# A state-space convolution and a gated unit in one kernel: the idle products of the head cut into halves of 256 columns

## The chip, the cores and the metric

The kernel runs on one core of a Trainium2 chip. A core has five engines that run side by side, each from an instruction stream of its own: TensorE (PE in the profile; its weight loads are listed apart, as PEld), VectorE (DVE), ScalarE (ACT), GpSimd (POOL) and SyncE (SP, which here only issues transfers). Sixteen DMA engines move data between the device's memory and the on-chip memories, and they also bring in the engines' code. TensorE writes its results to PSUM, a memory of eight banks, here two pairs and four single banks.

The metric is the device time of one execution in microseconds (us), the median over several runs. A profiled execution is a run of its own: it has a time, and a span from its first to its last instruction, and all rows of the profile count from the start of that span.

## The reference

Only what fixes the amount of work is shown.

```python
def reference(A_u, A_A_re, A_A_im, A_B_re, A_B_im, A_C_re, A_C_im,
              A_log_dt, A_Dskip, B_x, B_w_gate, B_w_up, B_w_down):
    # x is 1 x 2048 x 512 (bf16), F = 1792, 128 modes per channel
    x = A_u
    xn = _layernorm(x, axis=-1)
    return x + _A_ref(xn, ...) + _B_ref(xn, ...)

def _A_ref(u, ...):
    dt = jnp.exp(log_dt)[:, None]
    logdA = dt * (A_re + 1j * A_im)
    P = jnp.exp(logdA[:, :, None] * l)                # l = 0 .. 2047
    K = jnp.einsum("dn,dnl,dn->dl", Cc, P, dB).real   # one long filter per channel
    ...                                               # causal convolution of u with K by FFT
    return y + u * Dskip

def _B_ref(x, w_gate, w_up, w_down):
    g = jnp.einsum("bsd,df->bsf", x, w_gate)
    u = jnp.einsum("bsd,df->bsf", x, w_up)
    return jnp.einsum("bsf,fd->bsd", _sigmoid(g) * u, w_down)
```

So a normalized input goes through two branches, a long convolution and a gated unit with three matrix products, and both are added to the input.

## The kernel before

**The gated unit.** Its 2048 tokens are worked in four groups of 512. For each group and each of 14 blocks of 128 features there are four products with `wg_sb` (line 1036) and four with `wu_sb` (line 1060), each 128x128 against 512 columns. ScalarE takes the sigmoid and moves the other half out of PSUM (lines 1048 and 1072), VectorE multiplies the two (line 1076). Then, for each 128 tokens, 14 products with `wd_sb` (line 1105) sum into one bank.

**The convolution.** The filter is built from powers of a table on VectorE and ScalarE, and by four bursts of 128 small products on TensorE (line 820, `f_k`, 82 columns each, 64 to a call). The convolution itself is a transform of 2048 = 64 x 32, made by products (lines 694, 882, 904, 926, 985) with two passes through the device's memory in between (`z_scr` and `v_scr`), and pointwise products on VectorE.

**The head.** Four transfers bring the first tokens. VectorE and ScalarE compute the layernorm of the first 512 tokens, TensorE transposes them in two calls of eight (line 564, `ft`), and ScalarE and VectorE copy the transposes to `xnT` (lines 571 and 573). The weights come in by the queue of SyncE, `wg_sb` in three pieces and `wu_sb` in two, with more tokens in between.

**The idle products.** `keep_warm` (lines 516 to 522) adds an operation to TensorE's list that multiplies a zeroed tile, `glu_sb[:, 0, :]`, with itself into a PSUM bank that nobody reads. They compute nothing of the result; they only keep TensorE at work. There are eight such operations: one of 14 products, three of 3, and four of 1. In the order of TensorE stand the 14, a single one and a 3, then the first eight transposes, then a 3 and a single one, then the other eight transposes, then the last 3. Two single ones stand far behind, at 27.8 us and 194.0 us of the profile.

**The order of the work.** Every operation is added to a plan, and a list written out by hand, `ORDER`, gives the order in which the operations are issued; each engine takes its own in that order. PSUM banks and buffers are handed out in the same order. The cost given to `pl.add` is not used where `ORDER` is given. The number and the place of the operations don't depend on how many instructions one of them issues.

**The streams.** Each product is two instructions in TensorE's stream, a weight load and a product. The 1876 products of this kernel make 3752 instructions, and the code is brought in block by block while the kernel runs (queue 8 of the profile, kind "instruction").

Of the kernel before, what the change touches and what calls it, by code (L numbers as in the profile page):

```python
# [317 lines left out]
def kernel(  # L318
# [12 lines left out]
    V, S, T, P, Y = nc.vector, nc.scalar, nc.tensor, nc.gpsimd, nc.sync  # L331
# [12 lines left out]
    def bank(slot, r=0):  # L344
        if slot.pool == "s":
            return pairs[slot.idx][:, 512 * r:512 * r + 512]
        return banks[slot.idx][:]
# [18 lines left out]
    glu_sb = const.tile([128, 8, D], BF, name="glu_sb")  # L366
# [149 lines left out]
    def keep_warm(n, prio):  # L516
        wsl = _Slot("gu")

        def fn():
            for _ in range(n):  # L520
                T.matmul(bank(wsl), glu_sb[:, 0, 0:128], glu_sb[:, 0, :], start=True, stop=True)
        return pl.add("PE", 6.2 if n > 3 else 0.2155 * n, fn, (), prio, acq=[wsl], rel=[wsl])

    keep_warm(14, -10)
# [222 lines left out]
    for c in range(4):  # L747
        PC = PCH[c]
        cs = slice(CW * c, CW * c + CW)
# [9 lines left out]
        n = 1  # L759
# [435 lines left out]
```

## Time and profile before

| what | us |
|---|---|
| three runs | 217.63, 217.75, 219.24 |
| median | 217.75 |
| the profiled execution, its own time | 219.51 |
| its span, first to last instruction | 217.6 |
| TensorE busy | 209.0 |
| VectorE busy | 193.8 |
| ScalarE busy | 179.5 |

The busy times of the table can be read against the span: an engine with 96% has hardly any idle time, though ends of products are modelled, and two products that overlap in the pipeline count once. Between the span and the execution's own time lie 1.9 us before the first and behind the last instruction. The profiled execution was 1.8 us longer than the median of the three runs, so its rows are used for differences and not for the level.

### The profile page before, as it was taken

Reading aid. Unit: us, or ns where it says so; the run is one execution under the profiler, and the core shown is the slowest. Engines: PE = TensorE matmul, PEld = TensorE weight load, DVE = VectorE, ACT = ScalarE, POOL = GpSimd, SP = SyncE. Lnnn points to the kernel's source line nnn. Section 1 sums busy time; section 2 is a strip of 40 time slices with the busy share of each in tenths; the row PEclk is TensorE's granted clock in tenths of the full one; section 3 lists DMA queues with packets and bytes.
Section 4 is the critical chain, followed back from the end, with each engine's and each line's share of the span. In section 5 each row is a group of like instructions: output and inputs, shape, how many; then the busy total and the mean of one; then the engine's idle time right before and its main releaser. Section 6 shows DMA issues by size and latency. Waiting matters only on the chain.

```text
span 217.6 us, 4946 instructions
## 1 busy us (share of the span) xinstructions
PE 209.0 (96%) x1876; PEld 104.0 (48%) x1876; DVE 193.8 (89%) x438; ACT 179.5 (83%) x286; POOL 18.8 (9%) x40
## 2 busy tenths in 40 slices
PE   7979999999999999989999999999999999999894
PEld 2435444444444454435455565445546556544463
DVE  3989999999999999999999999999999999970433
ACT  3799999999999999869989999976897999960111
POOL 1410202002100020012000002010800000000000
PEclk9999999999999999999999999999999999999999
DMA  6999936001463689865697679929959969984974
GB/s 186 316 369 390 299 116 146 0 3 48 145 156 97 233 249 156 264 143 105 166 271 202 183 224 209 239 79 216 216 116 252 282 188 263 267 245 139 269 256 166
DMA packets 51530, 42.80 MB, mean 197 GB/s; under 512 B 16434, under 2 KB 43571, under 8 KB 51507
## 3 DMA queue, kind: packets, MB, share of 16 engines
q1 hardware_dynamic: 50338, 40.60, 63.8%
q0 software_dynamic: 864, 1.57, 5.5%
q10 hardware_dynamic: 304, 0.33, 0.6%
q8 instruction: 14, 0.23, 0.4%
q14 instruction: 10, 0.07, 0.1%
HBM read 25.97 MB, written 12.85 MB: 178 GB/s over the span
## 4 chain that ended last, share of the span: by engine, by line
PE 64%; DMA 17%; ACT 8%; SPq 7%; issue 2%; DVE 0%; ACTq 0%
PE bank L1060 18%; PE bank L1036 16%; PE bank L1105 10%; PE pair L904 7%; SPq L421 7%; DMA wu_sb<-in_B_w_up_dram 5%; PE pair L926 4%; ACT big L287 4%; DMA z_scr<-big 3%; DMA big<-big 3%; DMA big<-z_scr 2%; DMA v_scr<-big 2%; PE pair L882 2%; PE pair L820 2%; ACT us_sb L1072 2%
## 5 line engine op out<-in xcount | busy, mean ns | idle before, releaser
L287 ACT ACTIVATE big<-pair 128x1024 bf16<-128x1024 f32 x64 | 66.2, 1060 | 4.9 <-PE pair L926 1.5
L1060 PE MATMUL bank<-xnT,wu_sb 128*128 128x512 bf16 x224 | 54.5, 380 | 0.5 <-DMA wu_sb<-in_B_w_up_dram 0.4
L1036 PE MATMUL bank<-xnT,wg_sb 128*128 128x512 bf16 (+1 forms) x220 | 50.7, 368 | 1.9 <-DMA wg_sb<-in_B_w_gate_dram 1.8
L1105 PE MATMUL bank<-wd_sb,hT_sb 128*128 128x512 bf16 (+1 forms) x238 | 50.4, 367 | 0.0
L1036 PEld LDWEIGHTS <-wg_sb 128*128 128x128 bf16 x236 | 22.2, 98 | 26.9 <-issue 2.5
L1105 PEld LDWEIGHTS <-hT_sb 128*128 128x128 bf16 x238 | 22.6, 98 | 25.2 <-issue 1.9
L1060 PEld LDWEIGHTS <-wu_sb 128*128 128x128 bf16 x224 | 20.6, 98 | 25.2 <-issue 3.0
L1048 ACT ACTIVATE hT_sb<-bank 128x512 bf16<-128x512 f32 x52 | 30.9, 636 | 1.2 <-PE bank L1036 1.1
L735 DVE TENSOR_TENSOR big<-big 128x1024 bf16<-128x1024 bf16 (+4 forms) x40 | 26.8, 670 | 0.3 <-ACT big L287 0.2
L736 DVE TENSOR_TENSOR big<-big 128x1024 bf16<-128x1024 bf16 (+4 forms) x40 | 26.7, 667 | 0.0
L1072 ACT ACTIVATE us_sb<-bank 128x512 bf16<-128x512 f32 x40 | 25.9, 648 | 0.3
L909 DVE TENSOR_TENSOR big<-big 128x2048 bf16<-128x2048 bf16 x16 | 19.5, 1218 | 0.6 <-PE pair L926 0.3
L904 PE MATMUL pair<-big 128*128 128x256 bf16 x160 | 19.8, 273 | 0.0
L789 ACT ACTIVATE sq_sb<-big 128x256 bf16<-128x256 bf16 (+2 forms) x20 | 13.8, 691 | 5.1 <-DVE big L741 4.9
L904 PEld LDWEIGHTS <-big 128*128 128x128 bf16 x160 | 15.4, 98 | 4.9 <-issue 1.0
L1076 DVE TENSOR_TENSOR hT_sb<-hT_sb,us_sb 128x512 bf16<-128x512 bf16 x40 | 16.5, 418 | 0.4 <-ACT us_sb L1072 0.3
L740 DVE TENSOR_TENSOR big<-big 128x512 bf16<-128x512 bf16 (+4 forms) x40 | 16.5, 414 | 0.1
L741 DVE TENSOR_TENSOR big<-big 128x512 bf16<-128x512 bf16 (+4 forms) x40 | 16.5, 413 | 0.0
L1007 ACT ACTIVATE big<-pair 128x1024 bf16<-128x1024 f32 x3 | 3.1, 1023 | 15.2 <-PE pair L985 12.4
L895 DVE COPY big<-big 32x1024 bf16<-32x1024 bf16 x32 | 13.4, 419 | 0.6
L1011 DVE TENSOR_TENSOR big<-pair,glu_sb 128x1024 bf16<-128x1024 f32 x2 | 2.5, 1226 | 11.7 <-PE pair L985 8.1
L541 DVE BATCH_NORM_STATS2 stats<-big 128x6 f32<-128x512 bf16 x15 | 9.8, 682 | 3.4 <-DMA big<-in_A_u_dram 3.4
(104 smaller groups left out, 244.3 us busy)
## 6 DMA issues: line engine op xcount, KB each, us to landing
big<-c_E SPq DMA_DIRECT2D x16, 320.0 KB, 3.9
z_scr<-big SPq DMA_DIRECT2D x16, 256.0 KB, 2.9
big<-z_scr SPq DMA_DIRECT2D x16, 256.0 KB, 4.9
v_scr<-big SPq DMA_DIRECT2D x16, 256.0 KB, 3.1
big<-in_A_u_dram SPq DMA_DIRECT2D x4, 512.0 KB, 8.2
big<-big SPq DMA_DIRECT2D x32, 64.0 KB, 3.6
wu_sb<-in_B_w_up_dram SPq DMA_DIRECT2D x2, 896.0 KB, 10.7
wd_sb<-in_B_w_down_dram SPq DMA_DIRECT2D x1, 1792.0 KB, 15.1
```

The source lines that it names most:

```text
L287: nc.scalar.activation(out=get(out), in_=get(in_), func=ACT.Identity)
L735: V.tensor_tensor(out=wide(outp), in0=wide(lo), in1=mre, op=ALU.mult)
L736: V.tensor_tensor(out=wide(tb()), in0=wide(lo), in1=mim, op=ALU.mult)
L740: V.tensor_tensor(out=outp[:, :, 0], in0=outp[:, :, 0], in1=tb()[:, :, 1], op=opr)
L741: V.tensor_tensor(out=outp[:, :, 1], in0=outp[:, :, 1], in1=tb()[:, :, 0], op=opi)
L904: T.matmul(two(sk)[:, o:o + DW], es()[:, g, kt, :], kTv[p][:, :, kt, :], start=kt in (0, NKT - 1), stop=kt >= NKT - 2)
L909: V.tensor_tensor(out=pp().rearrange("p q h m -> p (q h) m"), in0=xx().rearrange("p q h m -> p (q h) m"), in1=kb()[:, 0:2 * DW].unsqueeze( ...
L1036: T.matmul(bank(sl, k % 2)[:, c0:c1], w[:, kt, k * 128:(k + 1) * 128], xnT[:, grp, kt, c0:c1], start=(kt == 0), stop=(kt == KT - 1))
L1048: S.activation(out=hT_sb[:, hs.idx, k % 2, :], in_=bank(sl), func=ACT.Sigmoid)
L1060: T.matmul(bank(sl), wu_sb[:, kt, k * 128:(k + 1) * 128], xnT[:, grp, kt, :], start=(kt == 0), stop=(kt == KT - 1))
L1072: S.activation(out=us_sb[:, us.idx, :], in_=bank(sl), func=ACT.Identity)
L1105: T.matmul(bank(po)[:, 0:c[1] - c[0]], hT_sb[:, hts[k // 2].idx, k % 2, jj * 128:(jj + 1) * 128], wd_sb[:, k, c[0]:c[1]], start=first and ...
```

## The change

The 14 and the three 3 are made of products of 256 columns instead of 512, in alternating halves of the bank and of the zeroed tile. The number of columns that stream through TensorE is the same. The four single ones stay as they are. The 14 + 3 + 3 + 3 = 23 products become 46 products, so TensorE's stream has 23 more weight loads and 23 more products, 46 instructions more, all of them ahead of 10.7 us. No operation is added, moved or taken away, so all other instructions have the order and the buffers that they had; behind the head each stands 46 places later in TensorE's stream.

```diff
@@ -517,8 +517,10 @@
         wsl = _Slot("gu")
 
         def fn():
-            for _ in range(n):
-                T.matmul(bank(wsl), glu_sb[:, 0, 0:128], glu_sb[:, 0, :], start=True, stop=True)
+            w = 256 if n > 1 else 512
+            for c in range(0, 512 * n, w):
+                cs = slice(c % 512, c % 512 + w)
+                T.matmul(bank(wsl)[:, cs], glu_sb[:, 0, 0:128], glu_sb[:, 0, cs], start=True, stop=True)
         return pl.add("PE", 6.2 if n > 3 else 0.2155 * n, fn, (), prio, acq=[wsl], rel=[wsl])
```

## The prediction

> **What bounds the kernel now.** I read the page first, then TensorE's waits, the stages, and the chain of waits. The page gives TensorE's share and the traffic of its code:
>
> ```profile
> PE 209.0 (96%) x1876; PEld 104.0 (48%) x1876; DVE 193.8 (89%) x438; ACT 179.5 (83%) x286; POOL 18.8 (9%) x40
> q8 instruction: 14, 0.23, 0.4%
> ```
>
> TensorE is busy nearly always, so what counts is where it still waits. The waits of TensorE's products (total, times, longest) and the busy times by stage (second number the length, then PE, PEld, DVE, ACT and POOL, then clock, DMA share and GB/s):
>
> ```profile
> PE bank L1036 <- DMA wg_sb<-in_B_w_gate_dram: 1.8, 1, 1.8
> PE pair L985 <- DMA big<-v_scr: 0.8, 1, 0.8
> PE pair L882 <- DMA big<-z_scr: 0.7, 1, 0.7
> PE bank L1060 <- DMA wu_sb<-in_B_w_up_dram: 0.4, 1, 0.4
> ```
>
> ```profile
> 12.50:21.30 8.80, 8.40 (x48) 4.62 (x48) 7.86 (x15) 8.50 (x14) 0.00 (x0) 1.00 1.06 380
> 21.30:96.50 75.20, 75.03 (x516) 33.44 (x517) 74.58 (x188) 72.46 (x126) 6.91 (x12) 1.00 0.55 148
> 96.50:201.00 104.50, 103.69 (x1157) 53.91 (x1155) 96.39 (x202) 87.95 (x134) 7.90 (x11) 1.00 0.76 202
> ```
>
> The reader is to see four waits, all for DMA, the first two of them by 21.3 us, and, between 21.3 and 96.5 us, TensorE and VectorE both full (75.03 and 74.58 of 75.20). A delay that reaches 21.3 us therefore goes to the end almost whole, and up to 21.3 us the DMA engines are the limit (share 1.06, all sixteen full). The chain of waits (start, length) shows two transfers on the path, `wu_sb` until 21.28 us (10.57 + 10.71) and a store of `v_scr`, and rows of products that are used below:
>
> ```profile
> 10.57 10.71 DMA wu_sb<-in_B_w_up_dram
> ...
> 30.78 5.18 PE bank L1060 x24
> ...
> 100.91 1.35 PE pair L820 x125
> ...
> 116.05 1.09 PE pair L904 x10
> ...
> 194.31 4.82 DMA v_scr<-big
> ...
> 202.30 0.52 PE pair L985 x6
> ```
>
> **The columns themselves.** The idle products stand in the head. The timeline there (start, length, engine, line) shows weight loads one product apart, then the first transposes, and the copies on ScalarE around them:
>
> ```profile
> 1.83 0.15 PEld L521 LDWEIGHTS <-glu_sb 128*128 128x128 bf16 x1 [0.28 <-issue]
> ...
> 6.95 0.15 PEld L521 LDWEIGHTS <-glu_sb 128*128 128x128 bf16 x1 [0.28 <-issue]
> 7.27 0.53 PEld L521 LDWEIGHTS <-glu_sb 128*128 128x128 bf16 x3 [0.17 <-issue]
> ```
>
> ```profile
> 6.66 0.73 DVE L553 TENSOR_SCALAR big<-big,ln_m_f,ln_ri_f 128x512 bf16<-128x512 bf16 x2
> 8.13 0.61 PE L564 MATMUL pair<-ident,big 128*128 128x128 bf16 x8
> 8.16 0.72 ACT L614 ACTIVATE big<-big,magic 128x512 f32<-128x512 f32 x1 [1.56 <-DVE ln_ri_f L495]
> 8.79 1.01 ACT L571 ACTIVATE xnT<-pair 128x1024 bf16<-128x1024 bf16 x1
> ```
>
> From 1.83 to 6.95 us lie twelve products, (6.95 - 1.83) / 12 = 427 ns each for 512 columns. Later in the kernel 24 of the same width take 5.18 us, 216 ns each. So the head runs at half pace up to about 7.2 us. At full pace ten products of 256 columns (L904) take 1.09 us, 109 ns each: two halves take 218 ns where one whole takes 216. About ten of the 23 split products run at full pace (the last of the first batch and two 3s): 10 x 2 ns = 0.02 us.
>
> At half pace the trace has no product of 256 columns. By columns two halves are 2 x 213 = 427 ns and cost nothing; no bound lies below that, since the columns still have to stream. The other end is a half whose weight load, 150 ns, doesn't hide behind the product before it: 213 + 150 = 363 ns. The 5.8 us from 1.4 to 7.2 us would then hold 16 halves, eight products instead of 13.6, and 5.6 products more would run later at 0.218, 1.2 us. I take zero: a load of 150 ns fits under 213, as at full pace the median load of 98 ns fits under 109:
>
> ```profile
> L904 PEld LDWEIGHTS <-big x160: 95/98/99, 112.8 to 188.5; 128*128 128x128 bf16 x160
> ```
>
> The transposes are covered by little. Their data is ready when VectorE's two scalings end, at 6.66 + 0.73 = 7.39 us; they start at 8.13 because the idle products stand ahead of them. ScalarE's copy L571 follows 0.05 us after they end (8.13 + 0.61 = 8.74), right behind L614. Were the idle products 1.2 us longer, that copy and ScalarE's work behind it would be 1.2 us late, while TensorE itself still has the 1.8 us wait for `wg_sb`. This is the price if the cover of the weight load is gone.
>
> **The stream.** 46 instructions more also move the code. Page and queue row give 3752 loads and products and 14 blocks of 0.23 MB / 14 = 16 KB; 3752 / 14 is about 268, so I estimate some 256 instructions to a block. Every block behind the head is now asked for 46 instructions, 23 products, earlier relative to the work. Windows cut around one such packet show when they come; 23.0 to 23.5, then 195.9 to 196.2:
>
> ```profile
> q8 instruction: 1, 0.02, 14.1%
> ```
>
> ```profile
> q8 instruction: 1, 0.02, 33.6%
> ```
>
> The share counts sixteen engines: 0.141 x 16 x 0.5 = 1.13 us on one engine, and 0.336 x 16 x 0.3 = 1.61 us. The second lies inside the last store of `v_scr`, on the path from 194.31 us. The page's median for that store is 3.1 us from issue to landing, against 4.82 here, and the DMA share behind the packet is telling:
>
> ```profile
> v_scr<-big SPq DMA_DIRECT2D x16, 256.0 KB, 3.1
> ```
>
> ```profile
> 195.90:197.20 1.30, 1.30 (x8) 0.59 (x7) 0.00 (x0) 0.00 (x0) 0.00 (x0) 1.00 0.88 232
> 197.20:198.20 1.00, 1.00 (x6) 0.49 (x5) 0.00 (x0) 0.00 (x0) 0.00 (x0) 1.00 0.69 196
> 198.20:199.20 1.00, 1.00 (x7) 0.45 (x5) 0.00 (x0) 0.00 (x0) 0.00 (x0) 1.00 0.13 48
> 199.20:200.40 1.20, 1.20 (x7) 0.53 (x6) 0.00 (x0) 0.00 (x0) 0.00 (x0) 1.00 0.02 9
> ```
>
> From 198.2 us on two of sixteen engines work (0.13 x 16), while the store is awaited until 199.13 us (194.31 + 4.82); I read the late one as the engine that was held up by the code. Where does the block come in the changed kernel? The products ahead of 196 us:
>
> ```profile
> 192.32 0.84 PE L926 MATMUL pair<-big 64*64 64x512 bf16 x16
> 193.09 1.04 PE L1060 MATMUL bank<-xnT,wu_sb 128*128 128x512 bf16 x4
> ...
> 195.03 6.22 PE L1105 MATMUL bank<-wd_sb,hT_sb 128*128 128x512 bf16 x28
> ```
>
> 23 products are 23 x 0.216 = 5.0 us among those of L1105, and about 2 us if they are the sixteen and the four of the first two rows. So the block comes at 191 to 194 us, ahead of the store or just at its start. At best the 0.8 us that TensorE waits at 202.3 goes: -0.8. At worst the engine stays busy through and nothing is won: 0. I take the middle, -0.4.
>
> The block of 23 us goes the other way. In the stage 12.5 to 21.3 us 48 products take 8.8 us, 0.183 each, so 23 of them are 4.2 us and the block comes at about 19 us, while `wu_sb` is awaited and all sixteen engines are full. If it falls on the engine that finishes `wu_sb` last, the landing at 21.28 us is up to 1.13 us later; on any other, nothing. I take +0.3.
>
> The Trainium skill, Runtime: NRT & Kernel Launch, section Instruction fetch mechanics, says that code comes in 16 KiB blocks by a queue of its own and that the cost of crossing into the next one is mostly hidden. By it the sum would be 217.75 us, with the two terms gone. The trace agrees on the size of the blocks, and its 4.82 us against 3.1 us speaks against "hidden" where the transfers are on the path.
>
> The sum: +0.02 + 0 - 0.4 + 0.3 = -0.1 us. The profiled execution's 219.51 (span 217.6) would become 219.4, and the median of 217.75 becomes **217.7 us**.
>
> **The rivals.**
>
> *Slower: a burst runs out of code.* The row of L820 shows 125 products in 1.35 us; 128 of them are a whole block by the estimate above. A block takes 1.0 us on its engine in the mean of the fourteen (0.004 x 16 x 217.6 / 14), and 1.6 at most in the windows above, besides the time to ask for it. If the shifted border lies just ahead of a burst, TensorE eats one block in 1.35 us while the next is still under way, and stands for 1 to 1.6 us; with two of the four bursts so, 2 to 3.2 us, 220.4 us. It decides from the point at which border and burst start lie closer than the work that TensorE has queued. For it: VectorE and TensorE are both full there, so nothing catches up. Against: in the profile before, no border does this, though there are four bursts, and TensorE's waits name only DMA of data.
>
> *Slower: the half pace lasts longer.* If halves count as less work for the clock, full pace comes later: if it lasts until the copy L571, the four idle products left at 7.2 us take 4 x 0.216 = 0.9 us more and the eight transposes behind them, now 0.61 us, some 0.4 more, so that L571 is 1.3 us late and the end, at worst, as much, 219.0 us. Against: the products of 256 columns in L904 run at full pace all along. The Trainium skill, TensorE: Matmul & The Clock Gate, Part 1, says that the gate watches activity in a window of about 3.4 us and doesn't count instructions; by it the halves would change nothing.
>
> *Faster: the tail cleared, the head not touched.* The -0.8 whole and no +0.3: 216.9 us, still within 1%. Only if other blocks free other transfers too, as that of `z_scr` (wait 0.7), does it go to 216.2.
>
> **How the numbers follow.** 1% is 2.2 us, about what a measurement here can tell from no change: faster is under 215.6, slower over 219.9. The forecast has 0.62, with a range of its own from 216.9 (-0.8) to 218.8 (+1.1). The faster rival has 0.16, and a third of that I leave for what lies under 215.6. The burst has 0.16, nearly all of it over 219.9; the clock 0.06, a third of it there. That makes faster 0.05, within 1% 0.78, slower 0.17. The range: 216.2 takes in the faster rival; above, 220.2 takes in the clock, the unhidden loads (217.7 + 1.2 = 218.9) with the `wu_sb` term (220.0), and half of the burst.
>
> **What would show it.** Right: weight loads of the idle products 213 ns apart up to about 7.2 us, transposes at about 8.1; the packet of queue 8 at 19 us instead of 23, and the last one ahead of 194 us; `v_scr` landing in under 4 us and no wait of L985. Wrong: loads 360 ns apart or transposes after 8.7; a gap inside a row of L820; a start of L1060 later than 22.4 us; a time outside the range.

## The result, and the profile after

The changed kernel takes 219.88 us (median of 15 runs, 218.62 to 223.30), the kernel before 218.34 us in the same comparison (15 runs, 217.59 to 223.09). The ratio is 1.0068, with a 95% interval from 1.0041 to 1.0096: the change makes the kernel about 1.5 us slower. In some executions of either kernel the mean granted clock of TensorE is lower and the time about 1.5 us longer or more; where medians of "full clock" are given below, they leave out the executions with a mean granted clock under 0.994. The changed kernel's is 219.77 us (11 runs).

Page and waits of the changed kernel, the lines that answer to those shown of before (its lines 904, 985, 1007 and 1060 are 906, 987, 1009 and 1062 here):

```profile
PE 210.4 (96%) x1899; PEld 107.3 (49%) x1899; DVE 194.2 (88%) x438; ACT 179.8 (82%) x286; POOL 15.8 (7%) x40
q8 instruction: 15, 0.25, 0.5%
```

```profile
PE bank L1038 <- DMA wg_sb<-in_B_w_gate_dram: 2.1, 1, 2.1
PE pair L906 <- issue: 0.7, 1, 0.7
PE bank L1062 <- DMA wu_sb<-in_B_w_up_dram: 0.3, 1, 0.3
ACT big L1009 <- DMA out_dram<-big: 4.7, 1, 4.7
```

There are 23 products more, as written. Two things are new: fifteen blocks of code instead of fourteen, and a wait of TensorE's for "issue", for nothing that the profile shows, in the middle of the L906 products. The wait of L987 for `v_scr` is gone. The last line stands against 2.8 us in the kernel before:

```profile
ACT big L1007 <- DMA out_dram<-big: 2.8, 1, 2.8
```

The profiled execution took 221.96 us, with a span of 219.8, and the stages of its head say why it is above the median:

```profile
12.50:17.00 4.50, 4.36 (x13) 1.71 (x14) 3.35 (x8) 4.30 (x7) 0.00 (x0) 0.63 1.08 367
17.00:21.30 4.30, 4.30 (x30) 2.68 (x28) 4.26 (x9) 2.79 (x5) 0.00 (x0) 1.00 1.05 393
```

The column behind the engines is the granted clock: 0.63 from 12.5 to 17.0 us, so half pace for most of it, 13 products where the next 4.3 us hold 30. TensorE had stood idle from 10.5 to 12.6 us, and the clock fell back at 13.6 us for 3.4 us. Four of the 15 executions have a mean clock about as low as this one's, 0.989, and so have many of the kernel before. The profile of before has no such fall, so the rows of the two from 12.5 to 23 us are not compared.

The halves themselves ran as in the prediction. The timeline of the weight loads:

```profile
2.04 3.99 PEld L523 LDWEIGHTS <-glu_sb 128*128 128x128 bf16 x19
```

The last of the 19 loads takes 0.15 us itself, so 18 steps in 3.84 us are 213 ns each, half of the 427 ns of before, and the transposes start at 7.97 us (8.13 before).

The new wait, in the timeline (start, length, engine, line):

```profile
131.42 1.42 PE L822 MATMUL pair<-big 128*32 128x82 bf16 x128
132.77 1.04 PE L1062 MATMUL bank<-xnT,wu_sb 128*128 128x512 bf16 x4
133.74 0.84 PE L928 MATMUL pair<-big 64*64 64x512 bf16 x16
134.51 0.61 PE L906 MATMUL pair<-big 128*128 128x256 bf16 x4
135.84 0.81 PE L906 MATMUL pair<-big 128*128 128x256 bf16 x6 [0.71 <-issue]
```

Ten products of one call are split into four and six. They depend on the same data, so it is no wait for data; the burst L822 has just run through 256 instructions, and a packet of queue 8 starts at 132.8 us, in the window 132.7 to 133.2:

```profile
q8 instruction: 1, 0.02, 19.2%
```

It takes 0.192 x 16 x 0.5 = 1.5 us. I read this as TensorE waiting for its next block of code; the runs below bear it out.

The end is the other place. The chain of waits after, then that of before:

```profile
210.02 1.03 ACT big L1009
211.05 0.02 issue
211.07 4.59 DMA out_dram<-big
215.66 0.02 issue
...
215.76 1.02 ACT big L1009
```

```profile
212.84 1.65 PE bank L1105 x14
214.49 0.02 issue
214.51 0.42 DVE big L1125
```

Before, the last products and an addition on VectorE end the kernel. After, ScalarE's last activation ends it; it needs one of three output buffers, and the store that frees this buffer takes 4.59 us. In the kernel before the median of such stores, from issue to landing, is 2.3 us:

```profile
out_dram<-big SPq DMA_DIRECT2D x7, 256.0 KB, 2.3
```

The stages of the changed kernel in that time:

```profile
212.50:213.50 1.00, 1.00 (x19) 0.88 (x16) 0.76 (x2) 0.00 (x0) 0.00 (x0) 1.00 0.31 115
213.50:215.00 1.50, 1.50 (x16) 1.29 (x14) 0.76 (x1) 0.00 (x0) 0.00 (x0) 1.00 0.18 51
```

The DMA share falls to 0.18, three of sixteen engines, while a store is awaited. In the window 212.3 to 212.8 the fifteenth block starts, 0.209 x 16 x 0.5 = 1.67 us on one engine:

```profile
q8 instruction: 1, 0.02, 20.9%
```

### The profile page after: what moved, and what is told of

Its sections match the earlier page's. It is cut to its first block, busy times and chain, and to the rows that moved or that the text cites. A ratio compares the mean times of both kernels' runs of the same rounds, so it can differ in the third digit from the quotient of the medians.

```text
span 219.8 us, 4992 instructions
## 1 busy us (share of the span) xinstructions
PE 210.4 (96%) x1899; PEld 107.3 (49%) x1899; DVE 194.2 (88%) x438; ACT 179.8 (82%) x286; POOL 15.8 (7%) x40
## 4 chain that ended last, share of the span: by engine, by line
PE 65%; DVE 18%; DMA 8%; SPq 4%; ACT 2%; issue 1%; ACTq 0%
PE bank L1062 17%; PE bank L1107 15%; PE bank L1038 13%; PE pair L906 8%; DMA wu_sb<-in_B_w_up_dram 6%; PE pair L928 5%; DVE big L738 5%; DVE big L737 5%; SPq L421 4%; DVE big L743 3%; DVE big L742 3%; DMA out_dram<-big 2%; DVE hT_sb L1078 2%; PE pair L884 2%; PE pair L822 1%; ACT big L1009 1%
## 5 line engine op out<-in xcount | busy, mean ns | idle before, releaser
L1038 PE MATMUL bank<-xnT,wg_sb 128*128 128x512 bf16 (+1 forms) x220 | 52.5, 377 | 2.2 <-DMA wg_sb<-in_B_w_gate_dram 2.1
L906 PE MATMUL pair<-big 128*128 128x256 bf16 x160 | 19.9, 273 | 1.0 <-issue 0.7
L906 PEld LDWEIGHTS <-big 128*128 128x128 bf16 x160 | 15.4, 98 | 6.1 <-issue 2.3
L287 ACT ACTIVATE big<-big 128x256 bf16<-128x256 bf16 x30 | 12.9, 465 | 0.0
```

Of the source, the lines that this page charges most:

```text
L287: nc.scalar.activation(out=get(out), in_=get(in_), func=ACT.Identity)
L906: T.matmul(two(sk)[:, o:o + DW], es()[:, g, kt, :], kTv[p][:, :, kt, :], start=kt in (0, NKT - 1), stop=kt >= NKT - 2)
L1038: T.matmul(bank(sl, k % 2)[:, c0:c1], w[:, kt, k * 128:(k + 1) * 128], xnT[:, grp, kt, c0:c1], start=(kt == 0), stop=(kt == KT - 1))
```

## The experiments

All but the five with a fourth output buffer at the end change only how many instructions stand where. Most use small products that nobody reads, with weights of 32 columns on a zeroed tile, put behind an idle product that is there already; a parameter says behind which and how many:

```diff
+            for c in range(pad):
+                t = 32 * (c % 4)
+                T.matmul(bank(wsl)[t:t + 32, 0:32], glu_sb[:, 0, 0:32], glu_sb[:, 0, 0:32], start=True, stop=True, tile_position=(0, t))
```

**The stream without the halves, at three places.** The kernel before, with 23 small products (46 instructions) behind the last idle products of the head, behind the single one at 28 us, or behind the one at 194 us:

```diff
-    keep_warm(...)
+    PADS = {3: 23}    # head; {4: 23} at 28 us; {5: 23} at 194 us
```

> The kernel before with its 512-column idle products as they were, and 23 small products (32x32 weights on a zeroed tile, 32 columns) behind the last of them in the head: 46 instructions at the place in the stream, without the halves. Theory S (the 46 places in TensorE's stream move the blocks of code): as the changed kernel, ratio to before 1.004 to 1.010, wu_sb lands about 1.4 us later than in the kernel before, a gap of about 0.9 us inside a row of L906's products at some 135 us, the last output stores late. Theory H (the halves themselves, by their pace or by the clock): ratio 1.000, within 0.002.

> The same 46 instructions put behind the single idle product at 27.8 us, so that the first block's border stays where it was. Theory S: wu_sb lands at about 21.3 us as in the kernel before, the gap at some 133 us and the late last stores stay; ratio 1.000 to 1.006, below that of the small products in the head by about 0.005 (1.1 to 1.4 us of 218). Theory H: 1.000. A third theory (C: only the wu_sb collision counts, the rest is absorbed): 1.000 here and 1.006 with the small products in the head.

> The same 46 instructions put behind the single idle product at 194 us: only the last border moves, and a fifteenth block is asked for. Theory S: wu_sb and the L906 products as in the kernel before; the last store of v_scr lands up to 1.5 us sooner (gain up to 0.8 us) and the fifteenth block holds up an output store (loss 1 to 1.7 us); ratio 0.997 to 1.007. Theories H and C: 1.000.

Measured: in the head 1.0074 (1.0033 to 1.0115), at 28 us 1.0087 (1.0048 to 1.0126), at 194 us 1.0108 (1.0082 to 1.0133). With no halves at all the loss is there, so theory H falls. The second falls less than I thought, and the third alone, above its expected range, is as slow as the others, so C falls too. The waits of the run in the head and of that at 28 us show the gap in the same products (L909 there):

```profile
PE pair L909 <- issue: 0.8, 1, 0.8
PE bank L1065 <- DMA wu_sb<-in_B_w_up_dram: 0.4, 1, 0.4
PE pair L990 <- DMA big<-v_scr: 0.2, 1, 0.2
ACT big L1012 <- DMA out_dram<-big: 5.0, 1, 5.0
```

```profile
PE pair L909 <- issue: 0.8, 1, 0.8
```

In the first, the wait for `wu_sb` is 0.4 us as in the kernel before, and its chain of waits has the transfer with the length of before:

```profile
10.56 10.70 DMA wu_sb<-in_B_w_up_dram
```

The packet came at 20.3 us there, while that transfer was still under way (it lands at 21.26), and cost nothing.

The second run shows more. Its fifteenth packet came at 211.8 us, yet in its profiled execution (219.19 us, the second lowest of seven) the last activation waits for its products and for no store:

```profile
212.13 1.02 ACT L1012 ACTIVATE big<-pair 128x1024 bf16<-128x1024 f32 x1 [2.69 <-PE pair L990]
```

So the late block doesn't cost in every execution.

The profiled execution of the third took 224.22 us, the longest of its six, and its timeline shows something that its 46 instructions can't have made, since they stand 38 us further on:

```profile
154.36 1.72 PE L825 MATMUL pair<-big 128*32 128x82 bf16 x125
159.04 0.22 PE L825 MATMUL pair<-big 128*32 128x82 bf16 x3 [2.96 <-issue]
```

TensorE stops for 2.96 us three products before the end of a burst. The stream up to there is that of the kernel before, so this can happen to it too: by the count of 256 a border lies just ahead of this burst. The places of the stops agree with this count. TensorE stops behind 1115 products, counted from the first, in the changed kernel and in the first two of these runs, and behind 1371 here: 256 products, two blocks of 256 instructions, further on in the stream.

**The halves, with a whole block more.** The changed kernel with 105 small products in the head: 46 + 210 = 256 instructions.

```diff
+    PADS = {3: 105}
```

> The changed kernel with its halves, and 105 small products more in the head, so that the stream has 46 + 210 = 256 instructions more, by the estimate one whole block, and all later borders lie where they lay in the kernel before. Theory S: no gap in L906, no late last stores; one block more is asked for in the head and may hold up wu_sb, ratio 1.000 to 1.006, below the changed kernel. Theory H: as the changed kernel, 1.007.

Measured: 218.72 us, ratio 1.0022 (0.9996 to 1.0048). The halves are there, the stream is 256 instructions longer, and the loss is not distinguishable from none. This speaks for the place of the borders and against the halves, and for blocks of 256 instructions; but the interval reaches that of the change, 1.0041 to 1.0096, and a sharper pair follows below (f1 and f4).

**Only the block at the end.** The 23 small products ahead of the products at 207 us, in `final` for its fourth pair (t == 3), behind the fourteenth border; the same with 105 small products in the head besides, so that the stream has a whole block more and no border in its last 46 instructions; 6 small ones at 194 us:

```diff
         def fi():
+            for c in range(23 if t == 3 else 0):
+                b = 32 * (c % 4)
+                T.matmul(bank(sl, 0)[b:b + 32, 0:32], ident[:, 0:32], ident[:, 0:32], start=True, stop=True, tile_position=(0, b),
+                         skip_group_check=True)
             for r in range(2):
```

> The kernel before with 23 small products (46 instructions) ahead of the products L999 at 207 us, behind the fourteenth border: all fourteen blocks come where they came in the kernel before, and only a fifteenth is asked for, some 46 instructions before the end. Theory T15 (the fifteenth block, in the output stores, is the loss): ratio 1.006 to 1.012, a queue-8 packet at 211 to 214 us, ScalarE's last activation waits over 4 us for an output store. Theory T14 (the loss comes from the border that moved ahead of 196 us): 1.000 to 1.002. Theory B (all borders of the body add up): 1.000 to 1.002.

> The same 23 small products at 207 us, and 105 more in the head (210 instructions), so that the stream has one whole block more: the borders of the body come 46 instructions later than in the kernel before, and none falls into the last 46 instructions. T15: 0.999 to 1.004, no queue-8 packet behind 205 us, although the products at 207 us are the same. If the 46 instructions cost their time by themselves: as the run with them alone.

> Six small products (12 instructions) behind the single idle product at 194 us: the fifteenth border lies some 12 instructions before the end instead of 46. T15: the block comes later, at 214 us or behind, when all but the last two output stores are out, and costs less: ratio 1.000 to 1.006. If any fifteenth block costs the same: 1.008 to 1.012. T14 and B: 1.000.

In this comparison 15 of 35 executions of the kernel before had a mean clock under 0.994, so I give medians of full clock, 218.14 us for the kernel before. The three ratios are 1.0045 (0.9998 to 1.0091), 1.0042 (1.0008 to 1.0076) and 1.0004 (0.9955 to 1.0053). The first, below the 1.006 that T15 asked for and by its interval not clear of none, has 219.41 us at full clock (8 runs): 1.3 above, with the wait that T15 names:

```profile
ACT big L1011 <- DMA out_dram<-big: 4.1, 1, 4.1
```

The second has 220.14 us (12 runs, 218.82 to 220.68), far from the 0.999 to 1.004 of T15 as I had written it. Its waits:

```profile
PE bank L1069 <- issue: 1.8, 1, 1.8
```

This is a new gap of 1.8 us at 102.4 us, between two products behind another burst and behind 861 products, 254 ahead of the 1115 above: with borders 46 instructions later this burst is the one that runs out of code. The last packet comes at 206.2 us and there is no long wait for a store at the end, but the run's time doesn't tell, since the other border moved with it. I had thought that borders that come later do no harm. The third is inconclusive: half of its 12 executions have such a low clock, the other half lie between 217.56 and 222.95 us. Its profile has a fifteenth packet at 216 us, so 12 instructions more suffice to have it asked for.

**The idle time of the head filled.** The spread by the clock hid the sizes, so I looked for a base without it: the kernel before with three more idle products and 125 small ones of 128 columns, one whole block in all, so that TensorE doesn't stand still before `wg_sb` lands:

```diff
-        keep_warm(3 if n < 3 else 1, -9 + n)
+        keep_warm(6 if n == 2 else 3 if n < 2 else 1, -9 + n, PADS.get(n + 1, 0))    # PADS = {3: 125}
```

> The kernel before with three more idle products of 512 columns and 125 small ones of 128 columns behind the last idle products: 256 instructions more, one whole block, and some 2 us of work that fills TensorE's idle time until wg_sb lands at 12.5 us. If that idle time lets the clock fall back in some executions (as from 13.6 to 17.0 us in the profile of the changed kernel): no granted clock under 0.995 in any run, fewer times over 220 us, ratio 0.996 to 1.000. If the clock doesn't depend on it: 1.000 to 1.003 and clocks of 0.989 as often as before.

Measured: 218.44 us, twelve runs from 217.96 to 218.67, no mean clock under 0.999, where the kernel before had 217.36 to 225.54 us in the same comparison (ratio 0.9991, 0.9959 to 1.0023). The theory of the idle time holds as far as this goes; over all runs below, 4 of 83 executions of kernels with the filled head had a mean clock under 0.994, against 41 of 128 of the kernel before, so the fall became rare and didn't vanish. The stages of the head show no idle time and full clock:

```profile
10.70:12.50 1.80, 1.80 (x110) 1.49 (x112) 1.80 (x4) 1.79 (x3) 0.78 (x5) 1.00 1.06 374
12.50:17.00 4.50, 4.50 (x52) 2.17 (x41) 4.12 (x9) 4.38 (x7) 0.00 (x0) 1.00 1.07 367
```

**The same questions on that base.** 46 instructions more in the head (all borders as in the change), 46 at 207 us (only the block at the end), 12 at 207 us, and halves with 26 small products fewer (the stream as in the base):

```diff
-    PADS = {3: 125}
+    PADS = {3: 148}    # f1; f2: 23 small ones at 207 us; f3: 6 there; f4: halves, {3: 99}
```

> Base: the kernel with the gap filled and one whole block more (218.44 us median, 217.96 to 218.67). Here 23 small products more in the same place, so the blocks' borders lie 46 instructions earlier in the work, as in the changed kernel, with no halves and no fall of the clock in the head. Theory S (the place of the borders is the whole loss): 219.6 to 220.4 us, median, every run over 218.8; a gap of about 0.9 us in L906's products and a last ScalarE activation that waits over 4 us for an output store. Theory K (the loss of the changed kernel is mostly the clock falling back): 218.3 to 218.8 us.

> The same base with 23 small products (46 instructions) at 207 us, behind the last border of the body: one block more is asked for in the last 46 instructions, and all others stay. Theory T15 (that block in the output stores): 219.2 to 220.0 us, 0.8 to 1.5 above the base, the last ScalarE activation waits over 4 us for an output store. If only the products' own time counts (23 at about 11 ns): 218.6 to 218.8.

> The same base with 6 small products (12 instructions) at 207 us: the block is asked for in the last 12 instructions and comes behind most output stores. T15 with the moment deciding: 218.4 to 218.8 us. If any such block costs the same: as with 46 instructions at 207 us. If the cost were in proportion to the instructions: about 0.3 us over the base.

> The same base with the idle products of the head in halves of 256 columns as in the change (26 products more) and 26 small ones fewer: the stream is again 256 instructions longer and all borders lie as in the base. Theory S: 218.2 to 218.7 us, as the base. Theory H (halves cost by themselves): 219.3 us or more.

| run | median us | range | over the base, 218.44 |
|---|---|---|---|
| 46 in the head (f1) | 220.18 | 219.85 to 221.28 | +1.74 |
| 46 at 207 us (f2) | 219.90 | 219.34 to 225.00 | +1.46 |
| 12 at 207 us (f3) | 219.07 | 218.50 to 223.00 | +0.63 |
| halves, stream as base (f4) | 218.15 | 217.58 to 225.03 | -0.29 |

The base was measured in the comparison before. In that of these four, f1 has the ratio 1.0105 (1.0078 to 1.0131) to the kernel before, and f4 1.0001 (0.997 to 1.0031).

The small products of the head take time of their own here, since nothing waits for `wg_sb` any more. The rows of the base, f1 and f4:

```profile
11.01 1.96 PE L526 MATMUL bank<-glu_sb 128*32 128x128 bf16 x125
```

```profile
11.37 2.25 PE L526 MATMUL bank<-glu_sb 128*32 128x128 bf16 x148
```

```profile
10.99 1.58 PE L528 MATMUL bank<-glu_sb 128*32 128x128 bf16 x99
```

So 0.29 us of f1's 1.74 is not the borders' doing, which leaves 1.45, and f4's gain of 0.29 is less than the 0.38 us by which its small products are shorter. S holds and K falls: without any fall of the clock in the head a loss of the size of the change's is there, and the halves with the borders in place cost next to nothing.

One thing that I expected of f1 didn't come. Its profiled execution took 220.19 us, as its median, and its last activation waits 4.1 us for a store, but the gap in the products of L909 is small:

```profile
134.29 0.81 PE L909 MATMUL pair<-big 128*128 128x256 bf16 x6 [0.20 <-issue]
```

So in that execution the end makes up most of the loss and the gap little.

Of f2's 1.46 us the small products' own time is small, 23 of them in the timeline:

```profile
206.09 0.32 PE L1005 MATMUL pair<-ident 128*32 128x32 bf16 x23
```

So about 1.46 - 0.32 = 1.14 us is the block. The activation's wait for an output store, f2's and then the base's:

```profile
ACT big L1016 <- DMA out_dram<-big: 4.0, 1, 4.0
```

```profile
ACT big L1012 <- DMA out_dram<-big: 2.8, 1, 2.8
```

Over all profiles with three output buffers and a block in the output stores this wait is 4.0 to 5.0 us in six, and in one, that of e2, there is none. Without such a block it is 2.8 us in four, 3.5 in e4, and there is none in e6 and f3.

With 12 instructions the block comes later, but it is not free. In the window 218 to 220 us of f3, whose page begins "span 216.9 us", the packet comes when all instructions are done:

```profile
q8 instruction: 1, 0.02, 3.2%
```

This execution took 219.49 us, 2.6 us more than its span. Two others of its eleven have 2.3 and 3.0 us, while every other execution of all these runs lies between 1.9 and 2.2. Perhaps an execution waits for the block at its end; this isn't shown, since in e7 the packet comes behind the last instruction too (216.1 us, span 215.6) and the execution took 2.0 us more than its span.

**By which way the block costs.** A fourth output buffer takes ScalarE's wait away without a change to the block; there is room for it in front of the input tile. It was tried on f1, on the base, on the changed kernel, on f2 and on the kernel before:

```diff
-    pl = _Plan(dict(s=NS, gu=NGU, hT=NHT, ..., ot=3, tg=2, us=2, sq=2))
+    pl = _Plan(dict(s=NS, gu=NGU, hT=NHT, ..., ot=4, tg=2, us=2, sq=2))
```

> The filled kernel with 23 small products more in the head (220.18 us median), and four buffers instead of three for the output tile, so that no activation waits for the store of three tiles before. Theory W (the block costs through that wait): ScalarE's last activation waits for no output store, 218.6 to 219.2 us, what is left over the base being the gap at some 134 us. Theory L (the block costs in the last stores themselves): 219.8 to 220.3 us.

> The filled kernel with one whole block more (218.44 us median), and four buffers for the output tile. Control for W and L: without a block at the end the wait is 2.8 us before the last activation, but VectorE's last addition ends later than it, so 218.0 to 218.5 us under both.

> The changed kernel with four buffers for the output tile and nothing else. W: 218.3 to 219.0 us in the executions with a granted clock of 0.995 or more, against 219.77 of the changed kernel and about 218.1 of the kernel before; L: 219.5 to 220.0.

> The filled kernel with 46 instructions at 207 us (219.90 us median with three output buffers), now with four. W: the block's 1.15 us go and only the small products' own 0.31 us stay over the control with four buffers (218.40): 218.6 to 219.0 us. If the block also costs in the last stores themselves: 219.3 to 219.8 us.

> The kernel before with four buffers for the output tile. W: its last activation waits 2.8 us but VectorE's last addition ends later, so 1.000, within 0.003, of the kernel before in the executions with a granted clock of 0.995 or more.

| kernel | three buffers | four buffers |
|---|---|---|
| base | 218.44 | 218.40 |
| block at the end alone (f2) | 219.90 | 218.88 |
| all borders as in the change (f1) | 220.18 | 219.40 |
| the changed kernel, full clock | 219.77 | 218.43 |
| the kernel before | | 218.05 |

The block alone costs 1.02 us less with the fourth buffer, and what is left over the control, 0.48 us, is near the products' own 0.32: W holds there. The columns of the table come from different comparisons. Against the kernel before at full clock in the same comparison, the base is 0.30 us slower with three buffers and 0.29 with four, f2 1.9 and 0.1, f1 2.3 and 1.3, so the reading is the same. In the timeline of the block alone with four buffers the last activation waits for its products, no more for a store, though the packet still comes at 212.2 us:

```profile
212.42 1.02 ACT L1016 ACTIVATE big<-pair 128x1024 bf16<-128x1024 f32 x1 [2.69 <-PE pair L990]
```

With the borders as in the change, 1.00 us stays over the control; this is more than I had expected. The small products' own time is 0.29 of it, and the rest is about the size of the gap in the L909 products, 0.7 us by the waits of that run:

```profile
PE pair L909 <- issue: 0.7, 1, 0.7
```

The changed kernel itself wins 1.3 us by the fourth buffer, its median of all twelve runs is 218.71. The kernel before with four buffers took 218.05 us, ratio 0.996 (0.9925 to 0.9996), where I had expected 1.000 within 0.003. That gain is doubtful, since the kernel before had 218.74 us at full clock in this comparison and 217.91 to 218.25 in the others. The base with four buffers took 218.40, from 218.12 to 219.35, with the ratio 0.9986 (0.9959 to 1.0014).

## Why the prediction was wrong

I forecast 217.7 us, no change; the kernel became 0.68% slower, about 1.5 us. The time lies inside the range, but the movement is clear of noise and the forecast had none.

**The columns: right.** Two halves cost what one whole does: 213 ns each at half pace, and f4 is no slower than its base (218.15 against 218.44 us, with 0.38 us less of small products). The bound of 1.2 us for a weight load that doesn't hide was not needed.

**The stream: the right mechanism, with the wrong blocks in the sum.** That the change acts by the borders of the code blocks is shown from both sides: 46 instructions without halves bring the loss (e1, f1), halves with a whole block more don't (e4, f4). Of the sum's two terms neither did what it was put in for. The +0.3 for `wu_sb` was nothing in e1, where the packet came while that transfer was under way. The block that the prediction put at 191 to 194 us came at 195.96 us in the changed kernel, and at 193.2 to 195.6 in the runs with the same borders. The -0.4 for `v_scr` is of the right kind, the wait of 0.8 us is gone in the changed kernel, but it was 0.2 us with the same borders in e1 and doesn't appear in the waits of the base (e8), whose last border lies as before. The 0.8 us was one execution's and no fixed part of the kernel.

**The step that failed** is the count: "Every block behind the head is now asked for 46 instructions, 23 products, earlier" moved fourteen blocks and didn't ask whether there would be fifteen. The stream ended so close to a border that 12 instructions more have another block asked for (e7), and with 46 it falls into the output stores, where it costs about 1.14 us by f2. The prediction had no term for it. The number of packets, 14, stood in the second row that I quoted; I didn't ask at which instruction a fifteenth would come.

**The first rival was right in kind, and priced too rarely.** A burst did run out of code, one of four, for 0.7 to 0.8 us in most of the profiles with these borders (0.4 with the change and four buffers, 0.2 in f1) and not 1 to 1.6. I had given this 0.16, since the profile before showed no such gap. That argument was weak: that no burst stopped in that execution was luck, and one of its borders is the place of a stop of 2.96 us in another (e3), with the same stream up to there.

**The second rival, the clock:** the halves don't prolong the half pace. Full clock came at 6.8 us in the profile of the change and at 7.1 us in that of before, and f4 with the halves is as fast as its base. But the clock does fall back, in the changed kernel's profile in the head, behind the idle time ahead of `wg_sb`, and by the mean clock in some executions of both kernels; filling that time made it rare. Whether the halves change how often it falls was not measured.

**The rule of the Trainium skill** (Runtime: NRT & Kernel Launch, Instruction fetch mechanics: crossing a border is mostly hidden) was the other way to get no change. Here two of fifteen blocks were not hidden: one because TensorE was through with a block before the next was there, one by a store on the path. Together they make up the 1.5 us, as far as the runs separate them.

**What stays open:** how the loss divides. In f1 it is 0.29 us of the small products, about 1.1 of the block and some 0.3 that is left, for the gap and whatever else. The gap is partly taken back further on. Weight load by weight load, the changed kernel with four buffers is 0.12 us behind the kernel before with four buffers at 132 us, 0.65 at 134 us and 0.14 from 165 us on; with f1 and its base, both with four buffers, the same three are -0.25, 0.57 and 0.33. These are single executions, so how much of the gap stays as a rule is open. By which engine the late block holds up a store was not seen: the profile doesn't say on which of the sixteen a packet lies, and in e1 a packet of 0.96 us goes with a store of 3.93. Why e3 is slower than e5, with the same late block, was not settled; its one profile has the stop of 2.96 us.

## What to carry to other kernels

Count instructions as well as columns. In this long unrolled stream the code arrives in blocks of 256 instructions, and an edit that adds instructions moves all later borders, to the good or bad of what they meet, so a small change of time may belong to the borders and not to the edit. A control costs little: the edit with its stream filled up to a whole block. Look at what stands around the last border, the shortest buffers of the tail and bursts of small instructions, before the edit itself is judged.

## What the runs showed of the hardware

A block of code is one packet, and it took 0.9 to 1.7 us in the profiles of the two kernels (2.6 in one case, in e3). A store that was under way when such a packet came took 4.59 us, instead of a median of 2.3 for output stores in the kernel before, with three of sixteen engines at work; I read this as the one engine with the packet holding up the whole store. In the changed kernel's profile TensorE stops after 4 products of L906, 128 products (256 instructions) behind a place in the burst: 4 + 16 + 4 products lie behind the burst, so 104 in it, and that border was passed at about 131.7 us (131.42 + 24 x 11 ns). The next block was usable at 135.84, some 4 us later, although its packet took 1.5; so the stop lies several calls behind the burst, in the middle of products that wait for nothing else.

In the profile of the change 2.1 us of idle time in the head (10.5 to 12.6 us) was followed by a fall of the granted clock for 3.4 us, from 13.6 to 17.0 us; in the profile of before 1.8 us of idle time was not. The Trainium skill, TensorE: Matmul & The Clock Gate, Part 1, gives about 3.4 us of idle time, one whole window, as what it takes. In this profile 2.1 us sufficed, and the measurement decides.
